# Sliding-window attention and a gated FFN: units of 192 tokens, q and k transposed on VectorE, and engine orders fixed by hand

## The chip, the core and the metric

The kernel runs on one core of a Trainium2 chip. The metric is the device time of one execution in microseconds (us). Five engines work side by side, each through its own row of instructions in order: TensorE (PE in the profile), VectorE (DVE), ScalarE (ACT), GpSimd (POOL) and SyncE (SP), which here only issues transfers. They wait for each other through semaphores.

## What is computed

```python
# q, k, v: 8 batches x 8 heads x 576 tokens x 64, float32
scores = scale * np.matmul(q, k.transpose(0, 1, 3, 2))
rel = pos[:, None] - pos[None, :]
mask = (rel >= 0) & (rel < 64)                  # causal window of 64
scores = np.where(mask, scores, -1000000000.0)
attn = exp(scores - max);  attn = attn / (sum(attn) + 1e-09)
out = np.matmul(attn, v)
x = out as 4608 tokens x 512                    # heads side by side
gate = np.maximum(x @ w_gate, 0.0)              # 512 x 1536
val = x @ w_val                                 # 512 x 1536
return gate * val @ w_out                       # 1536 x 512, float32
```

## The kernel before

Attention goes by batches of 576 tokens, each in three units of `U = 192` queries. With a window of 64, the queries of a unit see 256 keys, taken as two slices of 128 (`w` = 0, 1), each against 128 queries.

- Loads: five transfers bring each of q and k to `nat` (128 tokens on the partitions, 8 heads, pieces of 256 bytes), six bring v. GpSimd casts them to f16 (L119, L120, L128, L129).
- Transposes (L137): for each pair of heads TensorE turns five blocks of q and five of k; ScalarE copies `qT` out of PSUM (L141), VectorE copies `kT` (L143). Two heads lie one above the other, 64 partitions each.
- Scores (`st`, L155): a matmul contracts 64 rows (K = 64), the two heads of a pair in the two halves of the array. Keys lie on the output's partitions, queries on its columns.
- ScalarE takes the exponential (L162), without a maximum. GpSimd multiplies with a 0/1 `mask` (L164).
- `pv` (L174): `v` is the weight of 64 columns, and a second set of matmuls with ones as weight gives the sums of the rows, 64 times over. The two heads use the two halves of the columns.
- VectorE turns the sums by 32 x 32 blocks (L181), takes reciprocals of one column (L183), turns them back (L185) and multiplies (L191). The result is `xt`, which is already x transposed, as the FFN needs it.

The FFN goes by tiles of `TT = 512` tokens, nine in all. For each of 12 slices of 128 hidden units four matmuls with `wg` (L206) and four with `wv` (L209) go to two PSUM banks of the pool `h`, which has four; ScalarE applies the relu (L212), VectorE multiplies (L213) into `g_sb`. Then four groups of 12 `op` matmuls (L218), a copy on ScalarE (L221) and a store (L222).

The order within an engine is set by a scheduler from the program's order, which is attention of batch 0, weights, and then for each tile `attention(t + 1)` and `ffn(t)`. It puts an instruction of attention between FFN ones when its inputs are ready by the scheduler's own clock. The weights come in twelve transfers of 768 KB, through two staging buffers.

Of the kernel before, what the change touches and what calls it, by code (L numbers as in the profile page):

```python
# [9 lines left out]
FP32 = mybir.dt.float32  # L10
FP16 = mybir.dt.float16
ACT = mybir.ActivationFunctionType
MUL = mybir.AluOpType.mult


@with_exitstack
def kernel(
# [15 lines left out]
    HP = H // 2  # L33
    U = 192
    NU = S // U
    NC = DM // 128
    NF = DF // 128
    TT = 512
    scale = 1.0 / float(D) ** 0.5

    consts = ctx.enter_context(tc.tile_pool(name="consts", bufs=1))
    persist = ctx.enter_context(tc.tile_pool(name="persist", bufs=1))
    stage = ctx.enter_context(tc.tile_pool(name="stage", bufs=2))
    a_in = ctx.enter_context(tc.tile_pool(name="a_in", bufs=3))
    a_v = ctx.enter_context(tc.tile_pool(name="a_v", bufs=1))
    a_sb = ctx.enter_context(tc.tile_pool(name="a_sb", bufs=2))
    a_p = ctx.enter_context(tc.tile_pool(name="a_p", bufs=3))
# [4 lines left out]
    s_ps = ctx.enter_context(tc.tile_pool(name="s_ps", bufs=1, space=bass.MemoryType.PSUM))  # L52
    t_ps = ctx.enter_context(tc.tile_pool(name="t_ps", bufs=2, space=bass.MemoryType.PSUM))


    ident32 = consts.tile([128, 128], FP32)
    make_identity(nc, ident32)
    ident = consts.tile([128, 128], FP16)
    nc.vector.tensor_copy(ident, ident32)
    ones0 = consts.tile([128, 64], FP16)  # L60
    nc.vector.memset(ones0, 1.0)
    nc.vector.memset(ones0[0:64], 0.0)
    ones = consts.tile([128, 64], FP16)
    nc.vector.memset(ones, 1.0)


    mask = consts.tile([128, 2, 128], FP16)
    nc.gpsimd.memset(mask, 1.0)
    for w, (lo, hi) in enumerate(((64, -1), (0, 63))):
        nc.gpsimd.affine_select(  # L70
            out=mask[:, w], in_=mask[:, w], compare_op=mybir.AluOpType.is_ge, fill=0.0,
            base=lo, pattern=[[1, 128]], channel_multiplier=-1,
        )
        nc.gpsimd.affine_select(
            out=mask[:, w], in_=mask[:, w], compare_op=mybir.AluOpType.is_ge, fill=0.0,
            base=hi, pattern=[[-1, 128]], channel_multiplier=1,
        )
# [4 lines left out]
    kTs, v16s = [], []  # L82
    for i in range(2):
        kT = persist.tile([128, HP, 64 + S], FP16, name=f"kT{i}")
        nc.vector.memset(kT[:, :, 0:64], 0.0)
        kTs.append(kT)
        v16 = persist.tile([128, 2 * NU, H, 64], FP16, name=f"v16{i}")
        nc.vector.memset(v16[0:64, 0], 0.0)
        v16s.append(v16)

    def load_weights():
        for wt, src in ((wg, moe_w_gate), (wv, moe_w_val), (wo, moe_w_out)):
            n = wt.shape[1]
            step = n // 4
            sr = src.rearrange("(c p) n -> p c n", p=128)
            for c in range(0, n, step):
                stg = stage.tile([128, step, wt.shape[2]], FP32, name="stg")
                nc.sync.dma_start(stg, sr[:, c:c + step])
                nc.any.tensor_copy(wt[:, c:c + step], stg)  # L99

    xts = {}

    def xt_tile(t):
        if t not in xts:
            xts[t] = x_sb.tile([128, NC, TT], FP16, name="xt")
        return xts[t]

    def attention(b):
        kT, v16 = kTs[b % 2], v16s[b % 2]
        q16 = a_sb.tile([128, 5, DM], FP16, name="q16")  # L110
        k16 = a_sb.tile([128, 5, DM], FP16, name="k16")
        for src, dst in ((q, q16), (k, k16)):
            nat = a_in.tile([128, 5, H, 64], FP32, name="nat")
            for n in range(5):
                np_ = 128 if n < 4 else 64
                nc.sync.dma_start(  # L116
                    nat[0:np_, n],
                    src[b, :, n * 128:n * 128 + np_].rearrange("h p d -> p h d"))
            nc.gpsimd.tensor_copy(dst[:, 0:4], nat[:, 0:4].rearrange("p n h d -> p n (h d)"))  # L119
            nc.gpsimd.tensor_copy(dst[0:64, 4], nat[0:64, 4].rearrange("p h d -> p (h d)"))  # L120
        v_nat = a_v.tile([128, 2 * NU, H, 64], FP32, name="v_nat")
        for j in range(2 * NU):
            k0 = U * (j // 2) + (64 if j % 2 else -64)
            p0 = 64 if k0 < 0 else 0
            nc.sync.dma_start(  # L125
                v_nat[p0:128, j],
                v[b, :, k0 + p0:k0 + 128].rearrange("h p d -> p h d"))
        nc.gpsimd.tensor_copy(v16[64:128, 0], v_nat[64:128, 0])  # L128
        nc.gpsimd.tensor_copy(v16[:, 1:], v_nat[:, 1:])  # L129

        qT = a_sb.tile([128, HP, S], FP16, name="qT")
        for hp in range(HP):
            for w, (src, dst) in enumerate(((q16, qT[:, hp]), (k16, kT[:, hp, 64:]))):
                tp = t_ps.tile([128, S], FP16, name="tp", tag="tp")
                for n in range(5):
                    np_ = 128 if n < 4 else 64
                    nc.tensor.transpose(tp[:, n * 128:n * 128 + np_],  # L137
                                        src[0:np_, n, hp * 128:(hp + 1) * 128],
                                        ident[0:np_, 0:np_])
                if w == 0:  # L140
                    nc.scalar.copy(dst, tp)  # L141
                else:
                    nc.vector.tensor_copy(dst, tp)  # L143

        for u in range(NU):
            for h2 in range(HP // 2):
                st = s_ps.tile([128, 2, 512], FP32, name="st")
                for i in range(2):
                    hp = 2 * h2 + i
                    for w in range(2):  # L150
                        ks = U * u + 128 * w
                        qs = U * u + 64 * w
                        for e in range(2):
                            rows = slice(64 * e, 64 * e + 64)
                            nc.tensor.matmul(  # L155
                                st[:, e, (2 * i + w) * 128:(2 * i + w + 1) * 128],
                                kT[rows, hp, ks:ks + 128],
                                qT[rows, hp, qs:qs + 128],
                                start=True, stop=True)
                p = a_p.tile([128, 2, 2, 256], FP16, name="p")  # L160
                for e in range(2):
                    nc.scalar.activation(p[:, e].rearrange("p i c -> p (i c)"), st[:, e],  # L162
                                         ACT.Exp, scale=scale)
                    nc.gpsimd.tensor_tensor(  # L164
                        p[:, e], p[:, e],
                        mask.rearrange("p w c -> p (w c)")[:, None, :].to_broadcast([128, 2, 256]),
                        MUL)
                for i in range(2):
                    hp = 2 * h2 + i
                    pv = t_ps.tile([128, 2, U], FP32, name="pv", tag="tp")  # L170
                    for s in range(2):
                        for w in range(2):
                            for e in range(2):
                                nc.tensor.matmul(  # L174
                                    pv[64 * e:64 * e + 64, s, 64 * w:64 * w + 128],
                                    v16[:, 2 * u + w, 2 * hp + e] if s == 0 else (ones0 if u == 0 and w == 0 else ones),
                                    p[:, e, i, 128 * w:128 * w + 128],
                                    start=(s == 0 and w == 0), stop=(s == 1 and w == 1),
                                    skip_group_check=True)
                    sT = a_p.tile([128, U // 32, 32], FP32, name="sT")  # L180
                    nc.vector.transpose(sT.rearrange("p b c -> p (b c)"), pv[:, 1])  # L181
                    rT = a_p.tile([128, U // 32, 1], FP32, name="rT")
                    nc.vector.reciprocal(rT, sT[:, :, 0:1])  # L183
                    rs = a_p.tile([128, U // 32, 32], FP32, name="rs")
                    nc.vector.transpose(rs, rT.to_broadcast([128, U // 32, 32]))  # L185
                    q0 = b * S + u * U
                    while q0 < b * S + (u + 1) * U:
                        t = q0 // TT
                        q1 = min((t + 1) * TT, b * S + (u + 1) * U)
                        c0 = q0 - b * S - u * U  # L190
                        nc.vector.tensor_tensor(  # L191
                            xt_tile(t)[:, hp, q0 - t * TT:q1 - t * TT],
# [67 lines left out]
```

## Time and profile before

| | |
|---|---|
| three runs | 448.84, 449.08, 453.12 us (median 449.08) |
| profiled execution | 450.66 us, of which the span is 449.0 us |
| granted TensorE clock, mean | 0.975 |
| busy: TensorE, VectorE, ScalarE, GpSimd | 386.8, 184.3, 170.2, 171.8 us |
| moved | 39.85 MB read, 9.44 MB written |
| under 512 bytes | 121600 of 128802 packets |

The span is the time between the first and the last instruction of the profile. A row of a timeline has start, length, engine, line, operation, output<-inputs, shape and count. A row of a group has line, engine, operation, names, shapes and count, then the busy time in us and the mean of one in ns, then the engine's idle time just before and what ended it. A row of the windows has the stretch, its length, the busy time (and count) of PE, weight loads (PEld), DVE, ACT and POOL, the granted clock, the DMA engines' share and GB/s.

### The profile page before, as it was taken

The numbers are of one execution on the slowest core, as the hardware profiler recorded it, in microseconds if no ns is written. First come the engines' busy times: TensorE is split into PE (matmuls) and PEld (weight loads), VectorE is DVE, ScalarE is ACT, GpSimd is POOL, SyncE is SP. The second block draws the span as 40 slices with busy tenths as digits, with TensorE's granted clock in tenths as the row PEclk, the third lists the DMA queues.
The fourth block names the chain that finished last, engine by engine and source line by source line (L and its number), as shares of the span: only waits on it lengthen the run. The fifth ranks groups of instructions, "written<-read, shape, count | busy, mean of one in ns | idle before, by whom it ended". The sixth has DMA issues, their size and how long they took to land.

```text
span 449.0 us, 7194 instructions
## 1 busy us (share of the span) xinstructions
PE 386.8 (86%) x2768; PEld 188.1 (42%) x2768; DVE 184.3 (41%) x557; ACT 170.2 (38%) x284; POOL 171.8 (38%) x155
## 2 busy tenths in 40 slices
PE   0535789866889989998899889989999899999996
PEld 0313334433434444444444444444445444444442
DVE  1117234146349049505660385048614761330330
ACT  1235563531533254325432553255325522332322
POOL 4375022476278259525960593048003800000000
PEclk9999989976989999999999999999999999999999
DMA  9945889479931599159934960100011001101002
GB/s 182 263 129 168 255 229 242 103 176 207 215 80 30 142 224 210 36 147 224 195 58 111 220 105 2 69 26 2 0 51 45 2 1 47 48 0 71 25 0 93
DMA packets 128802, 49.74 MB, mean 111 GB/s; under 512 B 121600, under 2 KB 121600, under 8 KB 128768
## 3 DMA queue, kind: packets, MB, share of 16 engines
q1 hardware_dynamic: 128768, 49.29, 50.3%
q8 instruction: 21, 0.34, 0.4%
q14 instruction: 13, 0.11, 0.1%
HBM read 39.85 MB, written 9.44 MB: 110 GB/s over the span
## 4 chain that ended last, share of the span: by engine, by line
PE 66%; POOL 12%; SPq 7%; DMA 4%; ACT 4%; issue 3%; DVE 3%; ACTq 0%; POOLq 0%
PE op L218 19%; PE h L206 18%; PE h L209 18%; POOL p L164 9%; PE pv L174 7%; SPq L116 5%; PE tp L137 3%; ACT p L162 2%; DMA nat<-in_k_dram 2%; SPq L125 2%; PE st L155 2%; POOL v L129 2%; DMA stg<-in_moe_w_val_dram 1%; DVE rs L185 1%; DMA v_nat<-in_v_dram 1%
## 5 line engine op out<-in xcount | busy, mean ns | idle before, releaser
L164 POOL TENSOR_TENSOR p<-p,mask 128x512 f16<-128x512 f16 x96 | 108.2, 1152 | 125.0 <-ACT p L162 125.0
L206 PE MATMUL h<-xt,wg 128*128 128x512 f16 x432 | 119.7, 387 | 3.9 <-DVE xt L191 3.9
L209 PE MATMUL h<-xt,wv 128*128 128x512 f16 x432 | 120.0, 388 | 3.2 <-ACT wv L99 3.2
L213 DVE TENSOR_TENSOR g_sb<-r_sb,h 128x512 f16<-128x512 f32 x108 | 73.6, 684 | 106.4 <-PE h L209 100.6
L212 ACT ACTIVATE r_sb<-h 128x512 f32<-128x512 f32 x108 | 64.5, 598 | 96.9 <-PE h L206 95.2
L218 PE MATMUL op<-wo,g_sb 128*128 128x512 f16 x432 | 96.1, 379 | 0.0
L162 ACT ACTIVATE p<-st 128x512 f16<-128x512 f32 x96 | 52.2, 597 | 63.3 <-PE st L155 52.1
L174 PE MATMUL pv<-p,v 128*64 128x128 f16 x384 | 35.4, 247 | 32.0 <-POOL p L164 15.9
L218 PEld LDWEIGHTS <-g_sb 128*128 128x128 f16 x432 | 41.8, 98 | 50.0
L209 PEld LDWEIGHTS <-wv 128*128 128x128 f16 x432 | 40.2, 98 | 52.3 <-ACT wv L99 4.2
L206 PEld LDWEIGHTS <-wg 128*128 128x128 f16 x432 | 40.5, 99 | 48.2 <-issue 3.9
L181 DVE STREAM_TRANSPOSE sT<-pv 128x192 f32<-128x192 f32 x96 | 33.4, 368 | 53.5 <-PE pv L174 52.6
L143 DVE COPY kT<-tp 128x576 f16<-128x576 f16 x32 | 14.6, 457 | 90.2 <-PE tp L137 90.2
L221 ACT COPY o_sb<-op 128x512 f32<-128x512 f32 x36 | 21.1, 586 | 76.0 <-PE op L218 69.9
L174 PEld LDWEIGHTS <-v 128*64 128x64 f16 x384 | 20.7, 120 | 55.1 <-issue 32.2
L155 PE MATMUL st<-qT,kT 64*128 64x128 f16 x384 | 29.1, 234 | 5.0 <-ACT p L162 5.0
L141 ACT COPY qT<-tp 128x576 f16<-128x576 f16 x32 | 20.6, 644 | 33.4 <-PE tp L137 33.4
L191 DVE TENSOR_TENSOR xt<-pv,rs 128x192 f16<-128x192 f32 (+2 forms) x120 | 31.2, 298 | 0.3
L185 DVE STREAM_TRANSPOSE rs<-rT 128x192 f32<-128x192 f32 x96 | 30.3, 344 | 0.0
L174 PE MATMUL pv<-p,ones 128*64 128x128 f16 x384 | 29.2, 242 | 0.0
L137 PE MATMUL tp<-ident,q 128*128 128x128 f16 (+1 forms) x160 | 18.2, 227 | 9.7 <-POOL q L119 9.7
L119 POOL CAST k<-nat 128x2048 f16<-128x2048 f32 x8 | 15.1, 1889 | 28.5 <-DMA nat<-in_k_dram 28.5
(31 smaller groups left out, 161.2 us busy)
## 6 DMA issues: line engine op xcount, KB each, us to landing
v_nat<-in_v_dram SPq DMA_DIRECT2D x40, 256.0 KB, 5.0
out_dram<-o_sb SPq DMA_DIRECT2D x36, 256.0 KB, 2.1
nat<-in_q_dram SPq DMA_DIRECT2D x32, 256.0 KB, 4.8
nat<-in_k_dram SPq DMA_DIRECT2D x32, 256.0 KB, 5.1
stg<-in_moe_w_gate_dram SPq DMA_DIRECT2D x4, 768.0 KB, 5.1
stg<-in_moe_w_val_dram SPq DMA_DIRECT2D x4, 768.0 KB, 5.9
stg<-in_moe_w_out_dram SPq DMA_DIRECT2D x4, 768.0 KB, 5.1
nat<-in_q_dram SPq DMA_DIRECT2D x8, 128.0 KB, 4.3
```

What stands on the lines that cost most here:

```text
L137: nc.tensor.transpose(tp[:, n * 128:n * 128 + np_], src[0:np_, n, hp * 128:(hp + 1) * 128], ident[0:np_, 0:np_])
L155: nc.tensor.matmul(st[:, e, (2 * i + w) * 128:(2 * i + w + 1) * 128], kT[rows, hp, ks:ks + 128], qT[rows, hp, qs:qs + 128], start=True, st ...
L162: nc.scalar.activation(p[:, e].rearrange("p i c -> p (i c)"), st[:, e], ACT.Exp, scale=scale)
L164: nc.gpsimd.tensor_tensor(p[:, e], p[:, e], mask.rearrange("p w c -> p (w c)")[:, None, :].to_broadcast([128, 2, 256]), MUL)
L174: nc.tensor.matmul(pv[64 * e:64 * e + 64, s, 64 * w:64 * w + 128], v16[:, 2 * u + w, 2 * hp + e] if s == 0 else (ones0 if u == 0 and w == ...
L181: nc.vector.transpose(sT.rearrange("p b c -> p (b c)"), pv[:, 1])
L185: nc.vector.transpose(rs, rT.to_broadcast([128, U // 32, 32]))
L206: nc.tensor.matmul(h1, wg[:, c, fs], xt[:, c], start=(c == 0), stop=(c == NC - 1))
L209: nc.tensor.matmul(h2, wv[:, c, fs], xt[:, c], start=(c == 0), stop=(c == NC - 1))
L212: nc.scalar.activation(r_sb, h1, ACT.Relu)
L213: nc.vector.tensor_tensor(g_sb[:, f], r_sb, h2, MUL)
L218: nc.tensor.matmul(op, g_sb[:, f, ss], wo[:, f], start=(f == 0), stop=(f == NF - 1))
```

## The change

The kernel is written anew around units of 192 tokens, 24 in all, and around a `Weaver`: a heap of pieces of work with planned times. TensorE's FFN matmuls advance its clock (four matmuls of n columns count as `4 * n / 2400` us), and every piece whose time has come is written out before the next matmul group. `tc.manual_schedule()` keeps the order as written. So the rows of all engines are fixed by the planned times.

- q and k are loaded by units: partition `32 g + i` holds six neighbouring tokens of heads `2g` and `2g + 1`, in pieces of 1536 bytes. VectorE transposes 32 x 32 blocks (L184, four instructions a unit), which leaves 32 of a head's 64 dimensions on a group of 32 partitions. TensorE's transposes, their copies and the identity are gone.
- Scores (L199): K = 32, four groups of heads in four row tiles of the array, two halves of the dimensions (`dh`) added up in PSUM. 32 matmuls a unit instead of 16, in one group. Four banks, which `pv` takes over after them.
- The mask is multiplied on VectorE (L215). ScalarE copies `pv` out of PSUM (L239), and sums, reciprocals, back-transposes and normalizing (L244, L246, L252, L261) go once a unit over all four pairs of heads.
- FFN tiles of 512, ten times 384, and 256 tokens.
- Weights come in nine transfers of 1 MB in column slices, with three staging buffers, each cast half by GpSimd (L133) and half by ScalarE (L135). q of the first unit is issued by ScalarE, and q of the first three is cast there (L170).

VectorE between two FFN gates, in the middle of the program, before: `kT`, `sT`, `rs`, `xt` and `g_sb` as above, `h_1539` and the like being the FFN's PSUM banks.

```order
L213 TENSOR_TENSOR g_sb<-r_sb,h_1539 128x512
L181 STREAM_TRANSPOSE sT<-pv 128x192 x2
L183 RECIPROCAL rT<-sT 128x6 x2
L185 STREAM_TRANSPOSE rs<-rT 128x192 x2
L191 TENSOR_TENSOR xt<-pv,rs 128x192 x2
L213 TENSOR_TENSOR g_sb<-r_sb,h_1552 128x512
```

VectorE in the middle of the program now, from one unit's masks to its normalizing, with the next unit's transposes (`k_2885`, `q_2904`) among them.

```order
L215 TENSOR_TENSOR p<-p,mask 128x512
L299 TENSOR_TENSOR g_sb<-r_sb,h_2907 128x384
L184 STREAM_TRANSPOSE kT_94<-k_2885 128x2x6x32
L299 TENSOR_TENSOR g_sb<-r_sb,h_2975 128x384
L244 STREAM_TRANSPOSE sT<-xs 128x768
L246 RECIPROCAL rT<-sT 128x24
L184 STREAM_TRANSPOSE kT_94<-k_2885 128x2x6x32
L299 TENSOR_TENSOR g_sb<-r_sb,h_2994 128x384
L252 STREAM_TRANSPOSE rs<-rT 128x768
L299 TENSOR_TENSOR g_sb<-r_sb,h_3010 128x384
L184 STREAM_TRANSPOSE qT<-q_2904 128x2x6x32
L261 TENSOR_TENSOR xt<-xs,rs 128x4x192
```

The masks have come from GpSimd, the transposes from TensorE, and the work on the sums is in single long instructions between the gates.

VectorE at the start now, from the first unit's transposes to the third's (`k_150`, `k_211` and `k_319` are the k of the three units).

```order
L184 STREAM_TRANSPOSE kT_94<-k_150 128x2x6x32 x2
L184 STREAM_TRANSPOSE qT<-q_152 128x2x6x32 x2
L215 TENSOR_TENSOR p<-p,mask 128x512 x4
L184 STREAM_TRANSPOSE kT_94<-k_211 128x2x6x32 x2
L184 STREAM_TRANSPOSE qT<-q_213 128x2x6x32 x2
L215 TENSOR_TENSOR p<-p,mask 128x512 x2
L244 STREAM_TRANSPOSE sT<-xs 128x768
L246 RECIPROCAL rT<-sT 128x24
L215 TENSOR_TENSOR p<-p,mask 128x512 x2
L184 STREAM_TRANSPOSE kT_94<-k_319 128x2x6x32
L252 STREAM_TRANSPOSE rs<-rT 128x768
```

Each unit's transposes stand behind all masks of the unit ahead of it. ScalarE at the same place has, for the first and second unit, exponentials, the casts of q for the units that follow and the copies of `pv`.

```order
L211 ACTIVATE p<-st 128x512 x3
L170 CAST q_213<-qn 128x768
L211 ACTIVATE p<-st 128x512
L239 COPY xs<-pv 128x384 x2
L211 ACTIVATE p<-st 128x512
L239 COPY xs<-pv 128x384 x2
L211 ACTIVATE p<-st 128x512 x2
L170 CAST q_321<-qn 128x768
L211 ACTIVATE p<-st 128x512
```

The cast of the next q stands ahead of a unit's last exponential. On TensorE the first three units come one after another (32 `st`, 32 `pv`, three times), and then the FFN; in a tile of 384 tokens there are 24 FFN matmuls between a unit's `st` and its `pv`, and two units per tile. The pv of a tile's second unit stands in its `op` part, and 16, 24, 24, 28, then up to 36 `op` matmuls follow it before the next tile's `h`.

The core of the diff:

```diff
-    TT = 512
+    sizes = [512] + [384] * 10 + [256]
...
+    def u_trans(u, name, dh):
+        d = units[u]
+        src = d[name + "16"].rearrange("p (b e) -> p b e", e=64)[:, :, 32 * dh:32 * dh + 32]
...
+        nc.vector.transpose(dst.rearrange("p h (i j) -> p h j i", i=32),
+                            src.rearrange("p (h j) e -> p h j e", h=2))
...
+    def u_st(u):
...
+        for hh in range(2):
+            for w in range(2):
+                for dh in range(2):
+                    for g in range(G):
+                        rows = slice(32 * g, 32 * g + 32)
+                        nc.tensor.matmul(
+                            d["st"][g][:, (2 * hh + w) * 128:(2 * hh + w + 1) * 128],
+                            kT[rows, dh, hh, ks + 128 * w:ks + 128 * w + 128],
+                            d["qT"][rows, dh, hh, 64 * w:64 * w + 128],
+                            start=(dh == 0), stop=(dh == 1))
...
+    def u_mask(u, g):
+        p = units[u]["p"][g]
+        nc.vector.tensor_tensor(
+            p, p, mask.rearrange("p w c -> p (w c)")[:, None, :].to_broadcast([128, 2, 256]), MUL)
...
+    def plan_unit(u, T):
+        fast = u < UB
+        if not fast:
+            W.at(T - 22, lambda: u_load(u))
+        s = 0.5 if fast else 1.7
+        for i, (name, dh) in enumerate((("k", 0), ("k", 1), ("q", 0), ("q", 1))):
+            W.at(T - s * (4 - i), lambda name=name, dh=dh: u_trans(u, name, dh))
+        for i, name in enumerate(("k", "q", "v")):
+            W.at(T - s * 4 - (1.0 if fast else 4 - i), lambda name=name: u_cast(u, name))
+        W.at(T, lambda: u_st(u))
+        for g in range(G):
+            W.at(T + 0.8 + 0.6 * g, lambda g=g: u_exp(u, g))
+            W.at(T + 1.5 + 0.6 * g, lambda g=g: u_mask(u, g))
+        W.at(T + 4.4, lambda: u_pv(u))
+        for g in range(G):
+            W.at(T + 5.2 + 0.5 * g, lambda g=g: u_copy(u, g))
+        W.at(T + 7.6, lambda: u_sum(u))
+        W.at(T + 8.9, lambda: u_back(u))
+        W.at(T + 9.9, lambda: u_norm(u))
...
+        for u, T in enumerate((10.0, 15.3, 20.6, 46.0, 52.0)):
+            plan_unit(u, T)
+        for u in range(5, NU):
+            plan_unit(u, 64.0 + 13.2 * (u - 5))
+        W.advance(27.0)
+        for t in range(len(sizes)):
+            while normed[0] * U < starts[t] + sizes[t]:
+                W.pop()
+            ffn(t)
+        W.drain()
```

More of the change, by code (lines that the diff above doesn't have):

```diff
@@ L4 @@
 import concourse.tile as tile
[L5 to L6 removed]
+from concourse import mybir
 from concourse._compat import with_exitstack
@@ L101 @@
+    W = Weaver()
+    units = {}
     xts = {}
+    normed = [0]
     def xt_tile(t):
         if t not in xts:
[L105 removed]
+            xts[t] = x_sb.tile([128, NC, 512], FP16, name="xt")
         return xts[t]
[L108 to L141, printed above, removed]
[L142 to L196 removed]
```

302 lines of the change are left out of this document (221 added, 81 removed).

## The prediction

> **What bounds the kernel now.** I read first the page's head, for the busiest engine, and the window of the last five tiles, cut at the starts of the `op` matmuls that the chain of waits gives.
>
> ```profile
> span 449.0 us, 7194 instructions
> PE 386.8 (86%) x2768; PEld 188.1 (42%) x2768; DVE 184.3 (41%) x557; ACT 170.2 (38%) x284; POOL 171.8 (38%) x155
> ```
>
> ```profile
> 76.00 2.59 PE op L218 x12
> ...
> 435.06 10.37 PE op L218 x48
> ```
>
> ```profile
> 86.40:145.20 58.80, 47.99 (x432) 24.59 (x432) 31.72 (x113) 22.47 (x41) 40.12 (x34) 0.85 0.74 140
> ...
> 327.39:372.90 45.51, 43.09 (x330) 20.82 (x328) 22.22 (x68) 17.95 (x32) 13.54 (x12) 1.00 0.07 24
> 372.90:403.98 31.08, 31.08 (x145) 14.07 (x144) 8.25 (x12) 9.51 (x16) 0.00 (x0) 1.00 0.09 34
> 403.98:435.06 31.08, 31.08 (x145) 14.11 (x144) 8.25 (x12) 9.51 (x16) 0.00 (x0) 1.00 0.09 35
> ```
>
> TensorE is the bound, but not evenly. A window that holds only FFN work lasts 31.08 us for 512 tokens, 144 matmuls of 512 columns at 216 ns, with TensorE never idle. A window with one batch of attention in it lasts 45.51 us: 14.4 us more, of which only 2.4 us are idle. Nine tiles of 31.08 us are 279.7 us. The other 169 us are attention, waiting and the start: the first `op` matmul runs at 76.00 us, and the step from the first tile to the second (86.40 to 145.20) takes 58.8 us.
>
> ```profile
> 292.09 0.52 PE L137 MATMUL tp<-ident,q 128*128 128x128 f16 x5
> 292.54 0.53 PE L137 MATMUL tp<-ident,k 128*128 128x128 f16 x5
> 293.00 0.82 PE L206 MATMUL h<-xt,wg 128*128 128x512 f16 x3
> ...
> 295.70 0.30 PE L155 MATMUL st<-qT,kT 64*128 64x128 f16 x4
> 295.93 0.60 PE L209 MATMUL h<-xt,wv 128*128 128x512 f16 x2
> ...
> 305.20 0.40 PE L155 MATMUL st<-qT,kT 64*128 64x128 f16 x8
> 305.53 0.39 PE L209 MATMUL h<-xt,wv 128*128 128x512 f16 x1
> ...
> 312.14 0.30 PE L174 MATMUL pv<-p,v 128*64 128x128 f16 x4
> 312.27 0.28 PE L174 MATMUL pv<-p,ones 128*64 128x128 f16 x4
> 312.49 0.60 PE L206 MATMUL h<-xt,wg 128*128 128x512 f16 x2
> ```
>
> ```profile
> L206 PEld LDWEIGHTS <-wg 128*128 128x128 f16 x432 | 40.5, 99 | 48.2 <-issue 3.9 <-ACT wv L99 1.0
> ...
> L155 PE MATMUL st<-qT,kT 64*128 64x128 f16 x384 | 29.1, 234 | 5.0 <-ACT p L162 5.0
> ```
>
> Starts tell the cost, since the durations overlap (one `st` record has a mean of 234 ns). Five transposes take 0.45 us; eight sets per batch are 3.6 us. Four `st` matmuls take 0.23 us and eight take 0.33 us: 25 ns each plus about 0.13 us for the switch. Eight `pv` matmuls take 0.35 us, again about 27 ns each and 0.13 us. So the many small groups pay a switch each, and the transposes pay for themselves.
>
> **The change, part by part.** *FFN.* The same columns are multiplied, in one tile of 512, ten of 384 and one of 256 tokens. A `wg` or `wv` matmul of 384 columns should take 0.75 × 216 = 162 ns, if its weight load stays hidden; a load lasts 99 ns, so it does. Sum **279.7 us**, unchanged.
>
> *Transposes on TensorE:* removed, 8 × 3.6 = 29 us less of TensorE work.
>
> *Scores and `pv`.* Each of 24 units now has 32 `st` matmuls in one group, then, 24 FFN matmuls later (3.9 us), 32 `pv` matmuls in one group. `pv`: 32 × 27 ns + 0.13 + 0.1 on entry = 1.1 us. `st` has twice as many matmuls as before (768 for 384), each on a quarter of the rows. This trace has no four-way tile. Ends: half of today's 27 ns, were four at once to help as two do (32 × 13.5 = 0.43 us), and 54 ns, were they not to overlap (1.73 us). I take the nearest row, 27 ns: 0.87 + 0.23 = 1.1 us. 21 units lie beside the FFN: 21 × 2.2 = **46 us** (bounds 37 to 64).
>
> The Trainium skill, "TensorE: Matmul & The Clock Gate", section "Wait — 56ns, not 53.3ns?", says that one matmul's start never follows another's by less than about 25 ns, however small it is. This speaks against splitting K in two: by it `st` would be 32 × 25 = 0.8 us, and K=32 with twice the instructions buys nothing over K=64. The same page's "Part 3" gives 3.07× for four row tiles at 512 columns, by which `st` would be an estimated 0.58 us. The row that I use agrees with the first.
>
> *The start.* Here the three first units run alone, and the order of VectorE and ScalarE sets the pace.
>
> ```profile
> L162 ACT ACTIVATE p<-st 128x512 f16<-128x512 f32 x96 | 52.2, 597 | 63.3 <-PE st L155 52.1 <-PE pv L174 11.2
> L212 ACT ACTIVATE r_sb<-h 128x512 f32<-128x512 f32 x108 | 64.5, 598 | 96.9 <-PE h L206 95.2 <-DVE g_sb L213 1.5
> L221 ACT COPY o_sb<-op 128x512 f32<-128x512 f32 x36 | 21.1, 586 | 76.0 <-PE op L218 69.9 <-DMA out_dram<-o_sb 6.0
> L141 ACT COPY qT<-tp 128x576 f16<-128x576 f16 x32 | 20.6, 644 | 33.4 <-PE tp L137 33.4
> L213 DVE TENSOR_TENSOR g_sb<-r_sb,h 128x512 f16<-128x512 f32 x108 | 73.6, 684 | 106.4 <-PE h L209 100.6 <-ACT r_sb L212 3.2 <-ACT qT L141 1.3
> L185 DVE STREAM_TRANSPOSE rs<-rT 128x192 f32<-128x192 f32 x96 | 30.3, 344 | 0.0
> L191 DVE TENSOR_TENSOR xt<-pv,rs 128x192 f16<-128x192 f32 x72 | 22.1, 336 | 0.2
> L191 DVE TENSOR_TENSOR xt<-pv,rs 128x64 f16<-128x64 f32 x24 | 5.0, 206 | 0.0
> L183 DVE RECIPROCAL rT<-sT 128x6 f32<-128x6 f32 x96 | 14.9, 169 | 0.2
> L120 POOL CAST q<-nat 64x512 f16<-64x512 f32 x8 | 4.8, 606 | 4.1 <-DMA nat<-in_q_dram 4.1
> L119 POOL CAST q<-nat 128x2048 f16<-128x2048 f32 x8 | 15.1, 1888 | 21.6 <-DMA nat<-in_q_dram 21.6
> L99 ACT CAST wg<-stg 128x1536 f16<-128x1536 f32 x4 | 5.8, 1476 | 0.0
> L99 DVE CAST wo<-stg 128x1536 f16<-128x1536 f32 x1 | 1.0, 952 | 0.0
> ```
>
> VectorE's two L191 rows give 1.02 ns per element, and with it: transpose of 384 elements 344 + 196 = 0.54 us, of 768 elements 0.93; normalizing 768 elements 206 + 718 = 0.92; gate of 384 columns 684 − 131 = 0.55; reciprocal of 24 between 0.17 and 0.68, taken as 0.3. A mask multiply of f16 in SBUF on VectorE isn't in this trace: from 0.32 (512 elements at the rate of the L99 cast) to 0.68 (L213, the same operation and count); I take 0.68. ScalarE's copy of 384 columns: 586 − 0.9 × 128 = 0.47 (slope from L221 to L141); relu of 384, 0.48. A GpSimd cast of 768 columns: 0.82.
>
> ```profile
> 7.77 1.89 POOL L119 CAST q<-nat 128x2048 f16<-128x2048 f32 x1 [5.08 <-DMA nat<-in_q_dram]
> ...
> 49.32 1.91 PE L206 MATMUL h<-xt,wg 128*128 128x512 f16 x4
> 51.03 0.61 PE L209 MATMUL h<-xt,wv 128*128 128x512 f16 x1
> ```
>
> ```profile
> 10.00:15.00 5.00, 0.50 (x5) 0.16 (x2) 0.00 (x0) 0.64 (x1) 1.95 (x2) 1.00 1.36 210
> ...
> 20.00:25.00 5.00, 2.35 (x19) 1.35 (x18) 0.46 (x1) 2.12 (x5) 2.26 (x2) 1.00 0.93 331
> ```
>
> Now 1 MB is there at 7.77 us; the first unit's k and q are 0.79 MB, so at 210 GB/s its first cast starts near 6.5 us and its transposes near 7.4. Before TensorE has been dense for some us it runs at half speed: at 49.32 four matmuls of 512 take 1.71 us, 428 ns each and twice the 216 of later. So `st` takes 1.75 us in the start. One unit: transposes 2.2, `st` 1.75, four exps 2.4, a cast of the next q on ScalarE among them 0.8, last mask 0.7, some 0.3 of hand-over: 8.1 us. The next unit's transposes stand behind all four masks in VectorE's row, so the units don't overlap: the second starts at 15.5. With the first unit's sum and reciprocal among its masks and two ScalarE copies among its exps it takes 9, and the third starts at 24.5. That one's transposes stand among the second unit's L252 and L261 (1.9 us): `st` at 28.6, `pv` ends near 35, two weight casts (0.98 us each) and four copies bring it to 37.5, then 0.93 + 0.3 + 0.93 + 0.7: FFN starts at **40 us** (bounds 33 and 45). Input doesn't set this: three units are 3.9 MB and the first two weight slices 2.1 MB, 29 us at 210 GB/s and 18 at 331. The other slices and two more units, 10 MB, follow within 30 to 47 us, so by 48 to 76 us, and the first tile needs the last slice only in its `op` part, after 63 us. Its first 3 to 5 us run at half speed: **2.5 us**.
>
> *Waits that the fixed order adds.* Per unit in the FFN VectorE has 4 transposes 2.2, 4 masks 2.7, sum, reciprocal and back-transpose 2.2, normalizing 0.9, six gates 3.3: 11.3 us in a period of TensorE of (23.3 + 4.4)/2 = 13.9 us. It keeps up on the mean. But after `pv` it has 8.6 us of this (all but the masks) beside 48 matmuls of 7.8 us, and TensorE can run ahead of a gate only by the four banks of `h`, three matmul groups less the gate, 1.4 us. Before the second tile's `h` 16 `op` matmuls (3.5 us) stand against the chain copy, sum, back-transpose, normalizing of about 4.3; for the next tiles 5.2 against 5.5. `pv` waits for the fourth mask: 2.4 + 0.5 (a relu between) + 0.7 + 0.3 = 3.9 us after `st`, just the 3.9 us of cover. I allow 0.5 us per unit, **10 us**; ends 0 and 30.
>
> *The end* stays: after the last `op` row ends at 445.43 come 3.6 us of copy and store.
>
> Sum of the profiled execution: 40 + 279.7 + 2.5 + 46 + 10 + 3.6 = 381.8, and 1.7 for what lies outside the span (450.66 for 449.0). The median shown, 449.08, is 1.6 below that profiled run, so I give **382 us**.
>
> **Rivals.**
>
> *All of it hides better.* `st` at 13.5 ns (−9), no waits (−10), the start at 33 (−7): **356 us**. For it: the last FFN windows show TensorE with no idle at all when nothing blocks. Against: the 25 ns spacing, and three units that wait in one row.
>
> *VectorE becomes late.* It goes from 41% busy over 449 us to 81% in each unit, in a strict order, and any wait in that row falls on gates and masks alike. If casts on GpSimd (three per unit, 0.82 + 0.82 + 1.03 = 2.7 us) hold up the masks or the normalizing, half of it, 1.3 us a unit, reaches `pv`: 21 × 1.3 = 27 more, **409 us**. For it: the masks stand where the next unit's casts run, and `pv` has no cover left. Against: this trace shows no VectorE instruction with both inputs in SBUF, so no such hold-up. The Trainium skill, "SBUF — State Buffer", section "Who interferes with whom", states it as a rule: a VectorE instruction with two SBUF inputs and a GpSimd one that reads SBUF exclude each other for their whole length.
>
> *K=32 tiles run one after another*, so that the change doesn't do what it says: each `st` matmul then pays its latency instead of 27 ns. From 89 ns more each (68 us over 768) the kernel is slower than before; at the whole length of today's `st` record, 234 ns, it would be 768 × 0.207 = 159 us more, **541 us**. Against: the rows with eight above show two tiles overlapping fully (25 ns each, where 128 columns alone take 54).
>
> **How the numbers follow.** Forecast, 368 to 396: 0.52. Better hidden, 350 to 368: 0.20. VectorE late, 396 to 425: 0.17. Mixtures from 425 to 444: 0.05. Serial tiles: 0.06. The range 356 to 412 leaves out the last two, the lower part of the second and the upper part of the third, some 0.2. One per cent is about what a measurement of this kernel tells from no change; faster by more than that 0.93, within it 0.01, slower 0.06.
>
> **What would show it.** The starts of 32 `st` matmuls against the next FFN matmul: 1.1 us. First dense L309 near 40 us. The spacing of the last units' `op` groups, 27.7 us for 384 tokens, with idle time of TensorE before `pv` and `h` near 1 us in it. VectorE near 80% busy there. A mask much longer beside a GpSimd cast, or a gap before L226 over 1 us, would make the second rival right; an FFN start past 50 us would break my reading of the start.

## The result, and the profile after

The changed kernel takes **418.87 us** (median of 4 runs, 418.39 to 420.72), the kernel before 448.96 us beside it: a ratio of 0.932 (95% interval 0.927 to 0.937). It is faster, as forecast, but by 30 us where the prediction had 67, and above its range. The profiled execution took 418.46 us, with a span of 416.7.

The page's head and the shares of the chain that ended last:

```profile
span 416.7 us, 8098 instructions
...
PE 348.0 (84%) x3120; PEld 193.6 (46%) x3120; DVE 310.5 (75%) x448; ACT 188.3 (45%) x385; POOL 79.7 (19%) x103
...
PE 50%; DVE 32%; ACT 6%; issue 5%; DMA 5%; SPq 1%; POOL 0%; DVEq 0%; ACTq 0%; POOLq 0%
```

VectorE carries a third of the chain. The groups of instructions (busy us, mean ns of one, idle time before them) say with what:

```profile
L184 DVE STREAM_TRANSPOSE kT<-k 128x384 f16<-128x384 f16 x48 | 69.0, 1456 | 6.1 <-POOL k L172 6.1
...
L184 DVE STREAM_TRANSPOSE qT<-q 128x384 f16<-128x384 f16 x48 | 68.9, 1448 | 0.0
...
L215 DVE TENSOR_TENSOR p<-p,mask 128x512 f16<-128x512 f16 x96 | 41.3, 451 | 20.5 <-ACT p L211 19.7
```

A transpose of q or k takes 1.45 us; the prediction had 0.54. The 96 of them are busy for 138 us. TensorE's waits (us in total, times, longest), and its time before and after the FFN's start at 45.04 us (window, then busy time of PE, PEld, DVE, ACT and POOL, granted clock, DMA share, GB/s):

```profile
PE st L199 <- DVE qT L184: 33.9, 17, 11.7
PE h L309 <- DVE xt L261: 12.0, 7, 4.4
PE h L309 <- DVE g_sb L299: 7.6, 7, 1.2
PE pv L226 <- DVE p L215: 7.2, 8, 1.5
PE op L332 <- ACT r_sb L296: 4.2, 1, 4.2
```

```profile
0.00:45.04 45.04, 10.60 (x193) 8.28 (x194) 31.22 (x42) 18.06 (x32) 12.50 (x22) 1.00 0.76 206
45.04:413.10 368.06, 337.44 (x2928) 185.29 (x2927) 279.29 (x407) 169.66 (x353) 67.22 (x82) 0.97 0.40 109
```

From the FFN's start to the last matmul TensorE is idle for 368.06 − 337.44 = 30.6 us. The rows above hold the start's waits too; behind the FFN's start they are 11.1 us before `st` (a late transpose), 7.6 before `h` for a normalized tile and 7.6 for a gate, all of VectorE, and 4.2 before `op` for a relu of ScalarE. All of `pv`'s 7.2 us lie in the start.

The idle time is not the whole price. One wait in TensorE's timeline (start, duration, instructions, idle time before them), with two windows behind it:

```profile
234.54 0.23 PE L199 MATMUL st<-qT,kT 32*128 32x128 f16 x4
237.05 0.57 PE L199 MATMUL st<-qT,kT 32*128 32x128 f16 x28 [2.27 <-DVE qT L184]
237.56 0.85 PE L309 MATMUL h<-xt,wg 128*128 128x384 f16 x4
238.22 1.47 PE L309 MATMUL h<-xt,wv 128*128 128x384 f16 x4
239.47 1.49 PE L309 MATMUL h<-xt,wg 128*128 128x384 f16 x4
240.75 1.25 PE L309 MATMUL h<-xt,wv 128*128 128x384 f16 x4
```

```profile
237.00:238.20 1.20, 1.15 (x32) 0.80 (x32) 0.84 (x2) 0.57 (x2) 0.83 (x1) 1.00 0.00 0
238.20:241.84 3.64, 3.64 (x14) 1.74 (x12) 2.08 (x5) 2.37 (x6) 0.00 (x0) 0.53 0.01 2
```

TensorE waits 2.27 us, runs on for 1.2 us, and then four matmuls of 384 columns take up to 1.28 us from start to start instead of 0.66, at a granted clock of 0.53. The 2.27 us of waiting cost about another 1.7 (3.64 us at about half the work).

### The profile page after: what moved, and what is told of

It is laid out like the page before. It is cut to its first block, busy times and chain, and to the rows that moved or that the text cites. A ratio compares the mean times of both kernels' runs of the same rounds, so it can differ in the third digit from the quotient of the medians.

```text
span 416.7 us, 8098 instructions
## 1 busy us (share of the span) xinstructions
PE 348.0 (84%) x3120; PEld 193.6 (46%) x3120; DVE 310.5 (75%) x448; ACT 188.3 (45%) x385; POOL 79.7 (19%) x103
## 4 chain that ended last, share of the span: by engine, by line
PE 50%; DVE 32%; ACT 6%; issue 5%; DMA 5%; SPq 1%; POOL 0%; DVEq 0%; ACTq 0%; POOLq 0%
PE h L309 31%; PE op L332 12%; DVE qT L184 10%; DVE kT L184 6%; DVE sT L244 4%; PE pv L226 4%; DVE rs L252 4%; PE st L199 4%; DVE g_sb L299 3%; DVE xt L261 3%; ACT xs L239 3%; DMA kn<-in_k_dram 3%; DMA stg<-in_moe_w_out_dram 2%; ACT p L211 1%; DVE rT L246 1%
## 5 line engine op out<-in xcount | busy, mean ns | idle before, releaser
L309 PE MATMUL h<-xt,wg 128*128 128x384 f16 (+2 forms) x576 | 123.2, 338 | 18.4 <-DVE xt L261 12.0
L309 PE MATMUL h<-xt,wv 128*128 128x384 f16 (+2 forms) x576 | 122.7, 337 | 1.2 <-DVE g_sb L299 1.2
L299 DVE TENSOR_TENSOR g_sb<-r_sb,h 128x384 f16<-128x384 f32 (+2 forms) x144 | 80.0, 562 | 57.3 <-PE h L309 42.8
L296 ACT ACTIVATE r_sb<-h 128x384 f32<-128x384 f32 (+2 forms) x144 | 71.1, 494 | 97.6 <-PE h L309 86.0
L184 DVE STREAM_TRANSPOSE kT<-k 128x384 f16<-128x384 f16 x48 | 69.0, 1456 | 6.1 <-POOL k L172 6.1
L184 DVE STREAM_TRANSPOSE qT<-q 128x384 f16<-128x384 f16 x48 | 68.9, 1448 | 0.0
L215 DVE TENSOR_TENSOR p<-p,mask 128x512 f16<-128x512 f16 x96 | 41.3, 451 | 20.5 <-ACT p L211 19.7
L199 PE MATMUL st<-qT,kT 32*128 32x128 f16 x768 | 20.0, 228 | 34.1 <-DVE qT L184 33.9
L239 ACT COPY xs<-pv 128x384 f32<-128x384 f32 x96 | 40.0, 498 | 14.3 <-PE pv L226 14.3
L199 PEld LDWEIGHTS <-kT 32*128 32x128 f16 x768 | 13.1, 97 | 44.0 <-issue 31.6
L244 DVE STREAM_TRANSPOSE sT<-xs 128x768 f32<-128x768 f32 x24 | 23.6, 982 | 12.1 <-ACT xs L239 12.1
L261 DVE TENSOR_TENSOR xt<-xs,rs 128x768 f16<-128x768 f32 (+2 forms) x35 | 26.9, 794 | 0.1
```

The source lines that it names most:

```text
L184: nc.vector.transpose(dst.rearrange("p h (i j) -> p h j i", i=32), src.rearrange("p (h j) e -> p h j e", h=2))
L199: nc.tensor.matmul(d["st"][g][:, (2 * hh + w) * 128:(2 * hh + w + 1) * 128], kT[rows, dh, hh, ks + 128 * w:ks + 128 * w + 128], d["qT"][ro ...
L215: nc.vector.tensor_tensor(p, p, mask.rearrange("p w c -> p (w c)")[:, None, :].to_broadcast([128, 2, 256]), MUL)
L239: nc.scalar.copy(d["xs"][:, g], d["pv"][g])
L244: nc.vector.transpose(sT.rearrange("p g b c -> p g (b c)"), d["xs"][:, :, 1])
L261: nc.vector.tensor_tensor(xt_tile(t)[:, :, a - t0:z - t0], d["xs"][:, :, 0, a - lo:z - lo], rs[:, :, a - lo:z - lo], MUL)
```

## The experiments

Theory: the transposes are dear because each writes its 32 × 32 block with a step of six f16 elements (12 bytes), since token `6·i + j` stands in piece j; their 1.45 us make VectorE late, and everything else in the sum is about right. Rivals: TensorE itself is slower than reckoned (`st`, half speed); ScalarE's casts of the last weight slices hold up the gates; the masks don't belong on VectorE. Unless it is said otherwise a ratio is against the kernel before, and times in the text that are compared step by step are spans (416.7 for the changed kernel).

**1. Another order of writing, nothing else.**

```diff
-        nc.vector.transpose(dst.rearrange("p h (i j) -> p h j i", i=32),
+        if name == "q":
+            nc.vector.transpose(dst.rearrange("p h (b i j) -> p (h b) j i", i=32, j=2),
+                                src.rearrange("p (x j) e -> p x j e", j=2))
+            return
+        nc.vector.transpose(dst.rearrange("p h (j i) -> p h j i", i=32),
                             src.rearrange("p (h j) e -> p h j e", h=2))
```

k is written to adjacent elements, q to every second one. The number and size of all instructions and transfers stay; the tokens stand in another order, so that this kernel, like those of 2 and 5, takes scores and masks of other pairs of tokens and leaves out the attention that was asked for.

> Only the place to which VectorE's transposes (L184) write is changed: k to adjacent elements, q to every second one, where the changed kernel writes to every sixth (12 bytes apart). The tokens of a unit stand in another order for it, so scores and masks are of other pairs; every instruction keeps its size. Theory A: the step of 12 bytes is what makes these transposes 1.45 us; k's go to 0.55 us, q's to between 0.55 and 1.45, VectorE's load falls from 84% in the middle to about 60%, the waits of st on VectorE go, and the time is 375 to 390 us. Theory B: a transpose of 16-bit elements takes 1.45 us wherever it writes; time 415 to 420 us. Theory C: the order of the rows sets the time, not VectorE's load; transposes faster, but time above 405 us.

Measured: **372.58 us** (369.67 to 373.2), ratio 0.828 (0.824 to 0.832). The head, the shares of the chain, the transposes and two windows:

```profile
span 371.4 us, 8098 instructions
...
PE 334.7 (90%) x3120; PEld 189.7 (51%) x3120; DVE 230.9 (62%) x448; ACT 188.1 (51%) x385; POOL 79.9 (22%) x103
...
PE 78%; DMA 11%; DVE 4%; ACT 3%; SPq 2%; issue 1%; POOL 0%; ACTq 0%; POOLq 0%
...
L188 DVE STREAM_TRANSPOSE kT<-k 128x384 f16<-128x384 f16 x48 | 26.3, 552 | 6.0 <-POOL k L172 6.0
...
L185 DVE STREAM_TRANSPOSE qT<-q 128x384 f16<-128x384 f16 x48 | 27.9, 585 | 0.5 <-ACT q L170 0.5
```

```profile
0.00:36.42 36.42, 10.84 (x193) 8.29 (x193) 21.38 (x42) 18.37 (x32) 12.07 (x22) 1.00 0.91 263
36.42:367.80 331.38, 323.83 (x2928) 181.43 (x2927) 209.55 (x407) 169.16 (x353) 67.88 (x82) 0.99 0.44 121
```

The transposes fall to 0.55 and 0.585 us and 45.3 us of span go with them. The two kernels' windows divide these: 8.6 us in the start (45.04 against 36.42), 23.1 us of TensorE's idle time behind it (30.6 against 7.5), and 13.6 us of its busy time for the same 2,928 matmuls (337.4 against 323.8). Most of the last part is half speed at waits. From the FFN's start to the last matmul the changed kernel has six stretches at a granted clock of 0.50 (74.39 to 77.80, 91.45 to 98.28, 115.34 to 118.76, 238.22 to 241.64, 268.94 to 272.36 and 357.69 to 361.10 us), experiment 1 has one. The sum of the six, and that one (0.50 is its granted clock):

```profile
sum 23.91, PE 22.86 PEld 10.09 DVE 15.41 ACT 11.49 POOL 3.56; mean PE 3.81 PEld 1.68 DVE 2.57 ACT 1.92 POOL 0.59
```

```profile
65.11:71.94 6.83, 5.24 (x14) 1.67 (x14) 4.50 (x9) 3.97 (x7) 2.69 (x3) 0.50 0.44 103
```

At half speed half of TensorE's 22.86 and 5.24 busy us are lost, 11.4 and 2.6, which makes 8.8 of the 13.6. The other 4.8 are not divided by an experiment; an estimate puts most of them down to waiting that counts as busy: the four `st` before the wait above are shown as 0.23 us, some 0.17 more than four take at the 13.75 ns of experiment 5, and a group of `h` as 0.81 us where the next starts after 0.66. Some 25 waits at 0.16 us give 4 us.

VectorE's share of the chain drops from 32% to 4%. The theory holds, and the time is a little below the 375 to 390 us that it gave; the run also gives the price of the rest of the prediction's sum, below.

**2. How the price depends on the step.** As experiment 1, but q is written with `j=3` in place of `j=2`, a step of three elements.

> As the kernel with k written to adjacent elements and q to every second one, but q's transposes write to every third (6 bytes apart), tokens again in another order. Where between a step of 4 bytes (0.59 us) and of 12 (1.45 us) does the price come? If it grows with the step: some 0.75 to 0.9 us for q at 6 bytes. If there is a limit at one word of 4 bytes: 1.0 to 1.45 us. If the limit lies above: 0.6 us.

Measured in a single run: 374.41 us, and by groups:

```profile
L185 DVE STREAM_TRANSPOSE qT<-q 128x384 f16<-128x384 f16 x48 | 37.9, 796 | 0.5 <-ACT q L170 0.5
L188 DVE STREAM_TRANSPOSE kT<-k 128x384 f16<-128x384 f16 x48 | 26.3, 552 | 6.1 <-POOL k L172 6.1
```

So with a step of 2, 4, 6 and 12 bytes one transpose of 384 f16 columns takes 0.55, 0.585, 0.80 and 1.45 us. The price is one of the write pattern, and a step of two elements is nearly free.

**3. The masks back on GpSimd.** `nc.vector.tensor_tensor(p, p, mask…)` becomes `nc.gpsimd.tensor_tensor`.

> Only the mask multiplies go back from VectorE to GpSimd (four a unit, 1.15 us each there before, 0.45 on VectorE). Theory A (VectorE's load is the bound): VectorE is relieved of 1.8 us a unit, but a unit's fourth mask ends some 2 us later than now and pv waits for it; between 405 and 430 us. Theory C (cover between st and pv is what counts): pv waits 1.5 to 2.5 us in each unit, 440 to 470 us.

Measured: 440.57 us (439.55 to 440.63), ratio 0.980 (0.976 to 0.984), so 22 us slower than the changed kernel, though VectorE has 36 us less to do. Of its page and its waits:

```profile
L215 POOL TENSOR_TENSOR p<-p,mask 128x512 f16<-128x512 f16 x96 | 109.5, 1162 | 189.5 <-ACT p L211 189.3
```

```profile
PE pv L226 <- POOL p L215: 36.5, 44, 2.2
PE st L199 <- DVE qT L184: 27.5, 15, 11.8
```

A mask takes 1.16 us there against 0.45, four of them stand between the last `st` and `pv`, and `pv` waits 36.5 us in place of 7.2. Behind the FFN's start these are 21.0 us where there were none, about 1 us in each unit, while `st` waits 10.7 us there as before (11.1). With transposes of 1.45 us the time from `st` to `pv` is thus as much a bound as VectorE's load, and the move of the masks is worth 22 us of what the change brings. What it is worth beside cheap transposes was not tried.

**4. The casts of w_out.** ScalarE's cast of the first slice of `wo` waits 7.1 us for its transfer, ahead of relus, and TensorE's first `op` 4.2 us for those relus. Here GpSimd casts all of w_out: `if half == 0:` becomes `if half == 0 or wt is wo:`.

> Only the casts of w_out move from ScalarE to GpSimd. In the changed kernel's trace a cast that waits 7 us for its transfer stands in ScalarE's row ahead of relus, and the first op matmuls start 4.2 us late and at half speed. If that costs what it shows there: 5 to 6 us less, 412 to 415 us. If the units behind it are late anyway through VectorE: 416 to 420 us.

Measured: 414.16 us (411.51 to 415.4), ratio 0.921 (0.917 to 0.926); the `op` wait falls from 4.2 to 1.8 us, and what it waits for now is `wo` itself; the span falls by 3.0. `st` still waits 34.2 us. This is a side cost of a few us, not the cause.

**5. `st` issued twice.** Experiment 1 with `for dh in (0, 1, 0, 1)`, so 64 matmuls in a group. It measures what one four-way tile costs.

> As the kernel with k adjacent and q at every second element, but each st matmul is issued twice (64 a unit; scores count twice, for other pairs). TensorE is its bound, so the extra 32 matmuls of 21 units show in the time. At 13.5 ns each, as the spacing in the changed kernel's trace has it: 9 us more, 381 to 383 us. At the 27 ns of the prediction: 18 us more, 390 to 392. The Trainium skill, TensorE: Matmul & The Clock Gate, section Wait — 56ns, not 53.3ns?, gives a least distance of about 25 ns between starts; by it 17 us more.

Measured: 384.14 us (380.99 to 386.11), ratio 0.855 (0.849 to 0.861). Two groups in TensorE's timeline, first of experiment 1 and then of this kernel:

```profile
127.11 0.62 PE L203 MATMUL st<-qT,kT 32*128 32x128 f16 x32
127.67 0.82 PE L313 MATMUL h<-xt,wg 128*128 128x384 f16 x4
```

```profile
132.65 1.07 PE L203 MATMUL st<-qT,kT 32*128 32x128 f16 x64
133.65 0.82 PE L313 MATMUL h<-xt,wg 128*128 128x384 f16 x4
```

From start to start 32 take 0.56 us and 64 take 1.00: (1.00 − 0.56)/32 = 13.75 ns for each further matmul, and 0.12 us for the switch. Of the 13.0 us that the span grows by (384.4 for 371.4), 21 × 0.44 = 9.2 are these; 3.1 lie ahead of the FFN (its start moves from 36.42 to 39.48), where the expectation counted nothing. The 27 ns of the prediction were those of two tiles; four tiles halve them again.

**6. The whole computation with adjacent writes, in pieces of 256 bytes.** Piece j now holds tokens 32·j to 32·j + 31, so q and k are loaded in 256-byte pieces, by one transfer per head where one for two heads was.

```diff
-                        "h (i j) d -> i h (j d)", i=32))
+                for hh in range(2):
...
+                            "(j i) d -> i j d", i=32))
...
-        nc.vector.transpose(dst.rearrange("p h (i j) -> p h j i", i=32),
+        nc.vector.transpose(dst.rearrange("p h (j i) -> p h j i", i=32),
```

> The whole computation: q and k are loaded so that partition i holds the tokens 32 j + i (pieces of 256 bytes, two transfers where there was one), and the transposes write adjacent elements. Theory A: transposes 0.55 us, time 375 to 395 us, the start some us later or the same for the smaller pieces. Theory B: 415 to 425 us. Theory C: above 405 us.

Measured: 389.96 us (388.45 to 390.79), ratio 0.868 (0.864 to 0.871). The gain of the transposes is there, but the FFN starts at 44.95 us where experiment 1 has 36.42, and the first `op` waits 9.2 us for a relu of ScalarE.

**7. The same with 512-byte pieces.** Token `64·b + 2·i + j`: pieces of two tokens, and the transposes write every second element, the nearly free step.

> The whole computation: partition i holds the tokens 64 b + 2 i + j, loaded in pieces of 512 bytes (one transfer per head), and the transposes write to every second element. Transposes 0.55 to 0.6 us. If the 17 us between the two kernels with fast transposes (373 with pieces of 1536 bytes, 390 with 256 bytes) come from the size of the pieces at the start: some 378 us. If they come from having two transfers where there was one: 388 to 390 us.

Measured: 386.04 us (385.24 to 388.65), ratio 0.862 (0.857 to 0.866); transposes 583 to 585 ns, FFN start at 44.12. Larger pieces change the start little, and the time lies nearer the second expectation (388 to 390) than the first (378). SyncE's row in the start (start, time taken, transfers issued), of experiment 1 and then of this kernel:

```profile
0.81 1.80 SPq L146 DMA_DIRECT2D kn<-in_k_dram  x4
...
12.87 2.86 SPq L146 DMA_DIRECT2D qn<-in_q_dram  x4
...
16.88 0.97 SPq L126 DMA_DIRECT2D stg<-in_moe_w_gate_dram  x1
```

```profile
0.81 4.08 SPq L147 DMA_DIRECT2D kn<-in_k_dram  x8
...
10.36 3.74 SPq L147 DMA_DIRECT2D qn<-in_q_dram  x8
...
19.62 4.59 SPq L147 DMA_DIRECT2D qn<-in_q_dram  x8
...
25.36 0.78 SPq L126 DMA_DIRECT2D stg<-in_moe_w_gate_dram  x1
```

Eight transfers of half the size take 4.08 us to issue where four took 1.80. One of 48 KB takes 0.47 to 0.57 us in these rows, one of 96 KB 0.45 to 0.72, so that the number counts more than the size. SyncE issues 40 transfers of q and k ahead of the first weights where it issued 20, and these leave at 25.36 us and not at 16.88.

**8. Also the casts of w_out on GpSimd** (experiment 7 with the edit of 4).

> The same, and the casts of w_out on GpSimd. The trace of the kernel with adjacent writes has op waiting 6 us for a relu that stands behind such a cast, and TensorE is busy without a gap after 100 us, so here the wait counts in full: 5 to 9 us less than without. If what is late is w_out itself and not the relu: no difference, within 2 us.

Measured: 384.89 us (383.7 to 386.74), ratio 0.858 (0.854 to 0.861), the same as without it. The `op` now waits 8.7 us for `wo` itself: the transfer is late, and moving its cast doesn't help.

**9. Fewer transfers.** Layout of experiment 7, but q and k come by batch: four transfers per tensor for three units. Only unit 0 has its own, and units 1 and 2 share theirs.

```diff
+                        nc.sync.dma_start(
+                            nat[32 * g:32 * g + 32].rearrange("p h b e -> p (h b) e"),
+                            src[b, 2 * g:2 * g + 2].rearrange("h s d -> (h s) d").rearrange(
+                                "(x i j) d -> i x (j d)", i=32, j=2))
```

> The whole computation, as in the kernel with 512-byte pieces (386.0 us; its transposes write every second element), but q and k come by batch: four transfers per tensor for the three units of a batch, not eight per unit; only unit 0 has its own eight, and units 1 and 2 share theirs. Theory (SyncE's issue of about 0.47 us a transfer, whatever its size, holds up the start and the weights): SyncE issues some 12 transfers fewer ahead of the weights, 5 to 6 us, so the FFN starts near 39 to 41 us in place of 44.1, the first op waits 6 to 8 us in place of 9.2, and the kernel takes 376 to 382 us; transposes stay at 0.585 us and TensorE without idle between 100 and 350 us. Rival (the bytes or the size of the pieces hold up the start, not the number of transfers): the start stays at 43 to 45 us and the time at 384 to 388.

Measured: **376.13 us** (374.94 to 377.34), ratio 0.837 (0.834 to 0.841). SyncE's first weight slice, and the window from the FFN's start:

```profile
17.75 1.14 SPq L126 DMA_DIRECT2D stg<-in_moe_w_gate_dram  x1
```

```profile
40.02:371.30 331.28, 322.72 (x2928) 181.35 (x2927) 211.51 (x407) 169.01 (x353) 66.11 (x82) 0.99 0.56 121
```

The weights are issued at 17.75 us, the FFN starts at 40.02 as expected, and from there on it takes 331.3 us, as experiment 1 does. It starts 3.6 us later than in experiment 1, though the weights leave only 0.9 us later: the second unit's first `st` runs at 20.22 us where it ran at 15.76. The wait for w_out is 7.3 us, as long as expected, but stands elsewhere, before an `h`, since ScalarE's cast waits 9.4 us for the transfer:

```profile
62.80 1.86 PE L327 MATMUL h<-xt,wg 128*128 128x512 f16 x4 [7.33 <-ACT r_sb L314]
```

Like 6 to 8 this kernel does the whole computation, and it is some 73 us faster than the kernel before and 43 faster than the changed one.

**10. That wait taken off ScalarE's row**: experiment 9 with the edit of 4.

> The kernel that loads q and k by batch (376.1 us, span 374.9), with all casts of w_out on GpSimd. There ScalarE's cast of the first slice of w_out waits 9.4 us for its transfer with relus queued behind it; TensorE's h at 62.80 us waits 7.33 us for such a relu, and its next 10 matmuls run at half speed (about 2.2 us more). Theory (only ScalarE's row is in the way, since the first op would need the slice near 62.6 us and it lands near 61.2): the wait falls below 2 us, the half speed goes with it, and the kernel takes 366 to 369 us. Rival (as with 512-byte pieces and two transfers, where the same edit changed nothing, w_out itself is late, or its two more casts of 1.04 us per slice on GpSimd hold up k, q and v of the next units): a wait of 5 us or more stands before the first op or before an st or pv near 65 to 80 us, and the time stays at 373 to 377.

Measured: 375.57 us (374.46 to 376.38), ratio 0.833 (0.829 to 0.837), the same as experiment 9. The rival is right. GpSimd's row, with the idle time ahead of each piece of work, and then TensorE's next `st`:

```profile
62.10 2.02 POOL L133 CAST wo<-stg 128x1024 f16<-128x1024 f32 x2 [1.26 <-DMA stg<-in_moe_w_out_dram]
65.68 2.02 POOL L133 CAST wo<-stg 128x1024 f16<-128x1024 f32 x2 [1.56 <-DMA stg<-in_moe_w_out_dram]
67.65 0.83 POOL L190 CAST k<-kn 128x768 f16<-128x768 f32 x1
```

```profile
69.17 0.61 PE L217 MATMUL st<-qT,kT 32*128 32x128 f16 x16 [5.35 <-DVE kT L202]
```

The cast of the next k now stands behind four casts of w_out and their transfers, so its transpose comes late and `st` waits 5.35 us. As long as the transfers of w_out land where they do, some engine's row waits for them.

## Why the prediction was right and wrong

**The step that failed** is the price of a transpose: "transpose of 384 elements 344 + 196 = 0.54 us". It was taken from rows of f32 transposes of 32 × 32 blocks (192 elements), and the pattern that the new one writes wasn't compared with theirs. Measured: 1.45 us with the step of 12 bytes, and 0.55 us with adjacent writes, where the figure would have been right. The Trainium skill could have warned: "Vector Engine (DVE) Microarchitecture Reference", section "5.2 Measured stream behaviour on trn2 (trn3 not measured)", says that a port runs at full rate only on runs of adjacent pairs of 4-byte words, and gives 2.5 against 1.05 ns per column where the written stream steps by 24 words. By that ratio 0.55 us would become an estimated 1.3 us; the trace has 1.45. The page measured other operations, other steps and 32-bit data, and a step of 4 bytes between f16 elements, which experiment 1 has, cost almost nothing.

What followed from it, term by term:

- *VectorE per unit.* Predicted 11.3 us in a period of 13.9, "it keeps up on the mean". Four transposes at 1.45 add 3.6. In the stretch from 100 to 350 us it is busy 209.13 of 250, with masks cheaper than assumed (0.45 for 0.68). It is not full, but in its strict order a late transpose holds up `st`, and a late sum holds up `h`.

```profile
100.00:350.00 250.00, 229.35 (x2135) 127.77 (x2133) 209.13 (x306) 121.41 (x258) 47.10 (x58) 0.98 0.40 106
```

- *Waits, 10 us (0 to 30).* TensorE's idle time after the FFN's start is 30.6 us, just above the upper end, and the half speed that goes with waits was not in the sum at all: 11.4 us of lost time, against 2.6 in experiment 1. With the price that the prediction assumed the same stretch shows TensorE never idle:

```profile
100.00:350.00 250.00, 249.99 (x2378) 141.60 (x2377) 169.84 (x333) 133.25 (x283) 46.24 (x57) 1.00 0.39 107
```

- *The start, 40 us (33 to 45).* 45.04; with the cheap transposes 36.42. There the first unit's `st` comes at 9.63 us, where the chain has 7.4 + 2.2 = 9.6, but the third unit's at 23.65 for 28.6: the units behind the first were reckoned too long, and the 40 us were 3.6 too many.
- *Scores and `pv`, 46 us (37 to 64).* From its own first start `st` takes 0.56 us and `pv` 1.02 (243.66 to 244.68 us in the changed kernel); the way in from the FFN, which the prediction counts, adds 0.08 (four `h` matmuls ahead of `st` last from 233.80 to 234.54, 0.74 for 0.66). So `st` takes 0.64 and not 1.1, `pv` its 1.1: 21 × 1.74 = 36.5 us, just below the bounds, which is 9.5 us to the good. The lower end, 13.5 ns a matmul, was the right one; the row of two tiles was the wrong neighbour. The Trainium skill's rule that was weighed there ("TensorE: Matmul & The Clock Gate", section "Wait — 56ns, not 53.3ns?": about 25 ns from start to start at the least) does not hold across four row tiles, by the 13.75 ns of experiment 5. The 0.58 us estimated from the same page's "Part 3" comes near the 0.56 measured, in which 0.12 are the switch.
- *FFN, 279.7 us, its cold start and the end.* Held: at full speed four matmuls of 384 columns start 0.66 us from the next four (237.56 to 238.22 above), and the first 16, most of them at half speed, take 6.13 us (45.04 to 51.17) for 3.46, so 2.7 more for the 2.5 allowed. The granted clock reads 1.00 over this stretch all the same, so this half speed is read from the starts.

So the sum, 381.8, missed by 34.9: +5.0 in the start, −9.5 in `st` and `pv`, and the rest, 39.4, in waits (20.6 more than allowed), half speed (11.4) and, by subtraction, 7.4 of small gaps and waiting that counts as busy. The same sum against experiment 1, whose transposes cost what was assumed, is 10.4 too high: the start 3.6, `st` and `pv` 9.5, the waits 2.5 (7.5 us of idle time for 10), and against these some 5 us of busy time that it lacked, 2.6 of them half speed in the first `op` group and the rest, by subtraction, small gaps between groups. That the sum comes within 3% of experiment 1 thus rests in part on errors that cancel.

**The rivals.** "VectorE becomes late", 409 us, is what happened, and for another reason than the one named. GpSimd's casts do hold up a mask now and then. Engines at the second unit's first mask:

```profile
23.44 1.04 POOL L133 CAST wg<-stg 128x1024 f16<-128x1024 f32 x1 [2.34 <-DMA stg<-in_moe_w_gate_dram]
...
23.96 0.80 DVE L215 TENSOR_TENSOR p<-p,mask 128x512 f16<-128x512 f16 x1 [1.62 <-ACT p L211]
```

That mask takes 0.80 us and ends 0.28 us after the cast. This is near to what the prediction cites from the Trainium skill ("SBUF — State Buffer", section "Who interferes with whom"), but not the whole length, since the shortest mask takes 0.36 us. The 96 masks have a mean of 451 ns at a median of 421, so that all such hold-ups come to some 3 us of VectorE's time. "K=32 tiles run one after another" is refuted by experiment 5. "All of it hides better", 356 us, is not reached by any version; of its parts `st` at 13.5 ns and a steady stretch without idle time are there in experiment 1.

## What to carry to other kernels

Price an operation by a row with the same operand pattern, not only the same size: here the write step of a 16-bit transpose was worth 45 us of 449, and a layout that steps by two elements costs almost nothing while it still loads 512 bytes at a time. On TensorE a long wait also costs the half speed that goes with it; here 30.6 us of idle time had some 11 us of it beside them. In a start, count the transfers as well as the bytes: here one queue issued one in about half a microsecond.

## What the runs showed of the hardware that was not expected

- A transpose of 128 × 384 f16 on VectorE takes 0.55, 0.585, 0.80 or 1.45 us as its writes step by 2, 4, 6 or 12 bytes.
- Four row tiles of 32 rows overlap fully: 13.75 ns per matmul of 128 columns, a quarter of the 54 that 128 columns take alone (216 ns for 512).
- TensorE's granted clock falls to half at a wait of 2.27 us (238.20 to 241.84 us, 0.53). In the changed kernel each of the five waits of 2.25 to 4.16 us behind the FFN's start has 3.4 or 6.8 us at 0.50 with it, which begin between 1.1 us before the wait's end and 1.3 us after it. Of the 13 waits between 0.8 and 1.25 us only two have such a stretch (1.18 and 0.83 us, 1 us apart, ahead of 268.94); no wait between 1.25 and 2.25 us occurs. After a wait of 1.05 us the next groups still start 0.66 us apart, as TensorE's timeline of the changed kernel shows:

```profile
146.44 0.57 PE L199 MATMUL st<-qT,kT 32*128 32x128 f16 x28 [1.05 <-DVE qT L184]
146.95 0.82 PE L309 MATMUL h<-xt,wg 128*128 128x384 f16 x4
147.61 0.81 PE L309 MATMUL h<-xt,wv 128*128 128x384 f16 x4
```

- A transfer of q or k takes SyncE 0.45 to 0.72 us to issue in the first 25 us at 96 KB, and 0.47 to 0.57 at half of that.
